# Sliding-window attention with a dense layer: 75 of TensorE's waits stand at earlier products

## The chip, the cores and the metric

The kernel runs on one core of a Trainium2 chip. The metric is the device time of one execution in microseconds (us). Three runs of the kernel before gave 438.73, 439.21 and 439.93 us; their median, 439.21 us, is the time that the change is measured against.

## The reference

Two kinds of layer alternate, each twice over the same 2048 rows of 512 numbers, all in bf16: an attention with 32 heads of 16 and a causal window of 256 rows, and a dense layer with 1792 hidden columns. Cut to what matters:

```python
scores = einsum("bhqd,bhkd->bhqk", q, k) * (Dh ** -0.5)
mask = (i - j >= 0) & (i - j < 256)
p = softmax(where(mask, scores, -1e9))
o = einsum("bhqk,bhkd->bhqd", p, v)            # then o @ wo

x = x + A(layernorm(x))       # wqkv, window attention, wo
x = x + B(layernorm(x))       # gelu(x @ w1 + b1) @ w2 + b2
x = x + A(layernorm(x))
x = x + B(layernorm(x))
```

## The kernel before, in words

The rows are cut into 16 tiles of 128, two tiles make a block, and since both pairs of layers run over all rows there are 16 blocks (`NB`) for the attention. Layers are interleaved: while the attention of one block runs, the dense layer of earlier blocks and the layernorms and projections of later ones are worked off beside it.

Four kinds of product stand on TensorE (PE):
- dense products (`pe_group`, L666): projections to Q, K and V (`xnTA`, `Wqkv_sb`), the output projection (`Wo_sb`, `OT`), and the two products of the dense layer (`W1`, `W2`, both named `W_sb` in the profile, with `xnTB` or `gT`). They use the whole array of 128x128 and stream 512 or 256 columns;
- scores (`sc`, L767): K by Q with 32 rows of the array each, four side by side;
- products with V (`pv`, L819): the masked exponentials `E` by V, 64 rows by 17 columns of the array each, 128 of them in a row (64 in the first block of a layer). V lies there twice, as `Va` and shifted by half a tile as `Vs`;
- a few transposes (L652).

ScalarE (ACT) takes the exponentials out of PSUM (L774), VectorE (DVE) and GpSimd (POOL) multiply the masks in (L795), DVE turns the products with V out of PSUM (L828), POOL helps with the layernorm (L624, L630) and the normalisation (L836). SyncE (SP) issues the DMAs: the shifted copies `Vs<-Va` (L715), the transposes of the normalised rows (`xnTA<-xn`, `xnTB<-xn`, L645) and the loads and stores.

Nothing is scheduled at run time. A plan (`_Plan`) gathers some 3,080 steps as nodes with what they read and write; the table `_ORDER` gives the order in which they are issued, `_ALT` says which run on their second engine, `_BANKS` deals out the PSUM banks. `_TURNS` is a flat list of pairs of node numbers (a, z): z gets a dependency on a, by an invented resource that a writes and z reads:

```python
for a, z in zip(_TURNS[0::2], _TURNS[1::2]):
    nodes[a]["writes"] = nodes[a]["writes"] + ["turn%d" % z]
    nodes[z]["reads"] = nodes[z]["reads"] + ["turn%d" % z]
    nodes[z]["deps"].add(a)
```

The recording layer (`_Sched.op`) then goes through the nodes in `_ORDER` and works out which semaphores each has to wait for. It remembers for every engine which counts it has already waited for (`know`), and what the engine that raised that count knew itself (`snap`), so that nothing is waited for twice:

```python
for c, v in req.items():
    if self._acquire(eng, c, v):
        waits.append((c, v))
```

Each wait is recorded ahead of the node's first instruction (`e.wait_ge(s, v)`, L127). One wait rides on that instruction itself; the others become instructions of their own on the engine's sequencer (EVENT_SEMAPHORE, up to two waits each), which stand in front of it. On PE a product is a load of weights (LDWEIGHTS, engine PEld in the profile) and the matmul behind it, and the wait rides on the load. In the rows of the program's order below, "[waits ...]" names the counters that an instruction waits for, the ones in front of it included: `cnt_act`, `cnt_dve`, `cnt_pool` for the three engines, `cnt_spdma0` to `cnt_spdma7` for DMAs.

## Time and profile before

| | |
|---|---|
| median of 3 runs | 439.21 us (438.73 to 439.93) |
| profiled execution, its own time | 440.44 us |
| span in that profile, first to last instruction | 438.9 us |
| PE busy | 412.5 us, 94% |
| ACT busy | 386.6 us, 88% |
| DVE busy | 335.6 us, 76% |
| POOL busy | 209.1 us, 48% |
| mean granted TensorE clock | 0.998 |

A matmul's busy time in the profile is modelled and runs into that of the next, so a gap in PE's stream is better read from starts than from busy times: the start of a product, plus as many steps as there are products in the row, gives the time at which the next could start. A row of the timeline merges equal instructions that follow each other; its columns are the start, the time from the first start to the last end, engine, line, operation, what is written and read, shape, and the count; in brackets, how long the engine sat idle before it and what ended that. "issue" there means that the profile shows nothing that was waited for last. PEld is the load of weights, PEldq the sequencer in front of it.

### The profile page before, as it was taken

What the parts mean: (1) busy time and instruction counts of PE and PEld (TensorE: products, weight loads), DVE (VectorE), ACT (ScalarE), POOL (GpSimd) and SP (SyncE); (2) the same over time, 40 slices, a digit from 0 to 9 for tenths busy, and PEclk for the clock granted to TensorE, in tenths of its full rate; (3) what the DMA queues carried; (4) which work ended last, traced back from release to release, by engine and by line L of the source; (5) the groups of instructions that cost most, each with busy time, mean ns of one, the idle gap of its engine ahead of it and who ended that gap; (6) DMA issues with size and microseconds to landing.
All of it is one profiled execution on the core that took longest, in us unless ns stands there. A gap on an engine that the chain in (4) does not pass through costs nothing.

```text
span 438.9 us, 16863 instructions
## 1 busy us (share of the span) xinstructions
PE 412.5 (94%) x7497; PEld 227.9 (52%) x7571; DVE 335.6 (76%) x635; ACT 386.6 (88%) x458; POOL 209.1 (48%) x233
## 2 busy tenths in 40 slices
PE   8989999998699988999999999999999999999995
PEld 4555756554444544454454455454564554444662
DVE  6999878689867788976899687878877586655841
ACT  3999988999999899999999999999889989899442
POOL 4675263372555366731566344442443645635140
PEclk9999999999999999999999999999999999999999
DMA  7782812102300303212040111201322013003030
GB/s 234 216 210 39 221 32 52 38 21 40 58 3 13 52 4 46 32 34 44 10 94 2 25 27 28 52 1 33 43 55 50 1 31 82 7 0 76 3 108 25
DMA packets 49060, 23.51 MB, mean 54 GB/s; under 512 B 34268, under 2 KB 48988, under 8 KB 48988
## 3 DMA queue, kind: packets, MB, share of 16 engines
q1 hardware_dynamic: 48988, 22.43, 23.2%
q8 instruction: 60, 0.98, 1.0%
q14 instruction: 12, 0.10, 0.1%
HBM read 8.00 MB, written 2.10 MB: 23 GB/s over the span
## 4 chain that ended last, share of the span: by engine, by line
PE 76%; ACT 10%; DVE 6%; DMA 3%; issue 3%; POOL 1%; SPq 1%; POOLq 0%; DVEq 0%
PE ps L666 59%; ACT E L774 9%; PE ps L767 9%; PE ps L819 7%; DVE OD L828 1%; DVE KT L700 1%; POOL E L795 1%; DMA xnTA<-xn 1%; DMA xnTB<-xn 1%; DVE X L911 1%; DVE stat L618 1%; SPq L645 1%; ACT Va L609 0%; DMA X<-in_A_x_dram 0%; DVE E L795 0%
## 5 line engine op out<-in xcount | busy, mean ns | idle before, releaser
L774 ACT ACTIVATE E<-ps 128x1024 bf16<-128x1024 f32 x300 | 284.0, 1038 | 21.7 <-PE ps L767 20.2
L795 POOL TENSOR_TENSOR E<-E,mask 128x512 bf16<-128x512 bf16 (+2 forms) x112 | 121.6, 1097 | 107.7 <-ACT E L774 43.8
L666 PE MATMUL ps<-W_sb,gT 128*128 128x512 bf16 x415 | 106.5, 380 | 3.2 <-issue 2.5
L666 PE MATMUL ps<-xnTB,W_sb 128*128 128x512 bf16 (+1 forms) x542 | 105.5, 335 | 3.6 <-issue 1.6
L666 PEld LDWEIGHTS ps<-xnTB,W_sb 128*128 128x128 bf16 x560 | 52.0, 98 | 43.9 <-issue 4.3
L666 PE MATMUL ps<-xnTA,Wqkv_sb 128*128 128x256 bf16 x512 | 70.6, 273 | 2.2 <-DVE OD L828 1.1
L767 PE MATMUL ps<-QT,KT 32*128 32x128 bf16 (+3 forms) x1920 | 60.6, 231 | 4.9 <-ACT E L774 2.0
L795 DVE TENSOR_TENSOR E<-E,mask 128x512 bf16<-128x512 bf16 (+2 forms) x124 | 51.2, 438 | 14.1 <-ACT E L774 6.8
L666 PEld LDWEIGHTS ps<-W_sb,gT 128*128 128x128 bf16 x448 | 39.4, 98 | 43.1 <-issue 3.4
L828 DVE STREAM_TRANSPOSE OD<-ps 128x1024 f32<-128x1024 f32 x32 | 40.0, 1249 | 23.7 <-PE ps L819 23.5
L666 PEld LDWEIGHTS ps<-xnTA,Wqkv_sb 128*128 128x128 bf16 x512 | 46.3, 98 | 22.5 <-issue 3.2
L767 PEld LDWEIGHTS ps<-QT,KT 32*128 32x128 bf16 x1920 | 28.5, 92 | 51.3 <-ACT E L774 31.0
L899 ACT ACTIVATE gT<-ps,b1T 128x512 bf16<-128x512 f32 (+1 forms) x80 | 43.7, 606 | 10.1 <-PE ps L666 10.0
L907 POOL TENSOR_TENSOR Xb<-X,b2all 128x512 f32<-128x512 bf16 x32 | 36.8, 1152 | 20.4 <-DVE X L911 11.5
L618 DVE BATCH_NORM_STATS2 stat<-X 128x6 f32<-128x512 bf16 x64 | 43.3, 684 | 2.5 <-DMA X<-in_A_x_dram 1.7
L819 PE MATMUL ps<-E,Va 64*17 64x192 bf16 (+3 forms) x1920 | 39.9, 230 | 3.0 <-ACT E L774 1.3
L700 DVE TENSOR_TENSOR KT<-ps,parmask 128x1024 bf16<-128x1024 f32 x32 | 38.6, 1211 | 5.3 <-PE ps L666 5.1
L891 DVE TENSOR_SCALAR gT<-ps,b1T 128x512 bf16<-128x512 f32 (+1 forms) x60 | 36.8, 631 | 6.3 <-PE ps L666 5.9
L836 POOL TENSOR_TENSOR Nb<-OD,Rc 128x512 bf16<-128x512 f32 x18 | 19.0, 1056 | 42.9 <-DVE Rc L832 28.6
L819 PE MATMUL ps<-E,Vs 64*17 64x128 bf16 (+3 forms) x1920 | 39.2, 230 | 0.0
L630 POOL TENSOR_TENSOR rstd<-rstd,mhalf 128x2 f32<-128x2 f32 (+1 forms) x33 | 24.3, 736 | 28.9 <-DVE rstd L624 27.2
L911 DVE TENSOR_TENSOR X<-Xb,ps 128x512 bf16<-128x512 f32 x32 | 21.6, 682 | 19.2 <-PE ps L666 19.0
(49 smaller groups left out, 362.3 us busy)
## 6 DMA issues: line engine op xcount, KB each, us to landing
Vs<-Va SPq DMA_DIRECT2D x64, 68.0 KB, 2.9
W_sb<-in_B_w_dram SPq DMA_DIRECT2D x4, 512.0 KB, 4.6
out_dram<-X SPq DMA_DIRECT2D x16, 128.0 KB, 2.0
X<-in_A_x_dram SPq DMA_DIRECT2D x3, 512.0 KB, 6.6
Wqkv_sb<-in_A_wqkv_dram SPq DMA_DIRECT2D x4, 256.0 KB, 7.3
W_sb<-in_B_w_dram SPq DMA_DIRECT2D x1, 768.0 KB
W_sb<-in_B_w_dram SPq DMA_DIRECT2D x2, 384.0 KB, 5.2
Wqkv_sb<-in_A_wqkv_dram SPq DMA_DIRECT2D x1, 512.0 KB, 6.9
```

The source lines that it names most:

```text
L618: add("dve", lambda e, B, t=t, k6=k6: e.bn_stats(stat6[:, k6, :], X[:, t, :]), reads=["X%d" % t], writes=["st%d" % k6], key="bs%d" % (k + j))
L666: r = e.matmul(ps[:, B[g][0], cols], lhsT, rhs, start=st, stop=sp)
L700: add("dve", lambda e, B, g=g, i=i: e.tensor_tensor(out=KT[:, kb, 2 * i : 2 * i + 2].rearrange("p c m a q -> p a (c m) q"), in0=ps[:, B[g] ...
L767: x = e.matmul(ps[:, bk[r], o : o + n], KT[rows, kb, c, m].rearrange("p a q -> p (a q)"), QT[rows, c, q : q + n], start=True, stop=True)
L774: add("act", lambda e, B, g_=g_, gi=gi: e.activation(E[:, 2 * gi : 2 * gi + 2, e0 : e0 + 512], ps[:, B[g_][0] : B[g_][0] + 2, :], AF.Exp, ...
L795: fn = lambda e, B: e.tensor_tensor(out=Ew, in0=Ew, in1=Mw, op=ALU.mult)
L819: x = e.matmul(ps[32 * r : 32 * r + VW, B[g][par], c % 2 * 2 * P + lo : c % 2 * 2 * P + hi], V[rows, (2 * b + m // 2) % VR, c * HC + 2 * r ...
L828: add("dve", lambda e, B: e.transpose(OD[:, s].rearrange("p a c q -> p (a c q)"), ps[:, B[g][0] : B[g][0] + 2, :]), reads=["ps:" + g], wri ...
L891: add("dve", lambda e, B, g=g, fc=fc: e.tensor_scalar(out=gT[:, fc, c0 : c0 + M], in0=ps[:, B[g][0], 0:M], scalar1=b1T[:, fc : fc + 1], sc ...
L899: add("act", lambda e, B, g=g, fc=fc: e.activation(gT[:, fc, c0 : c0 + M], ps[:, B[g][0], 0:M], AF.Gelu_apprx_tanh, bias=b1T[:, fc : fc + ...
L907: add("pool", lambda e, B, t=t, xs=xs: e.tensor_tensor(out=Xb[:, xs, :], in0=X[:, t, :], in1=b2all[:], op=ALU.add), reads=["X%d" % t, "b2a ...
L911: add("dve", lambda e, B, g=g, t=t, xs=xs: e.tensor_tensor(out=X[:, t, :], in0=Xb[:, xs, :], in1=ps[:, B[g][0], :], op=ALU.add), reads=["X ...
```

## The change

75 pairs are added to `_TURNS`. In each, the first node is one that TensorE waits for in any case at a later node, and the second is a dense product that stands ahead of that later node in `_ORDER`. The dense product now waits, and by `know` the later node no longer does. No instruction is added, left out or moved on any engine; only waits are. Of the 75, 63 are for DMAs, 7 for POOL and 5 for DVE. 54 of them stood at the first product with V of a group (19 places), 2 at scores, 19 at first products of a dense group (15 places). They now stand at 64 products of 512 columns and 11 of 256; 70 of these are not the first of their group. TensorE has 649 waits before and after. The products that carry a wait on themselves go from 436 to 511, the wait instructions that stand alone on PE at L127 from 161 to 119, 28 of the 42 in front of products with V. On SP four DMA transposes no longer wait for an earlier DMA of their own counter, because what they wait for otherwise now implies it.

```diff
@@ -358,7 +358,14 @@
     2817, 2842, 2751, 2751, 2945, 2945, 2940, 2945, 2944, 2944, 2935, 2935, 2958, 2935, 2954, 2954, 2962, 2954, 2949,
-    2995, 2889, 2995, 2906,
+    2995, 2889, 2995, 2906, 149, 233, 148, 231, 141, 168, 45, 263, 44, 246, 426, 320, 646, 537, 579, 294, 186, 293,
+    441, 301, 905, 627, 903, 625, 364, 679, 365, 678, 358, 509, 555, 742, 967, 823, 682, 862, 674, 846, 1282, 894,
...
+    2514, 2350, 2516, 2345, 2536, 2329, 2591, 2333, 2785, 2384, 2429, 2383, 2423, 2381, 2422, 2380, 2430, 2361, 2795,
+    2683, 2543, 2748, 2549, 2743, 2542, 2742, 2843, 2722, 2841, 2721, 2954, 2862, 2998, 2903,
 ]
```

The first place is PE around 186 us of the profile, ahead of a group of products with V. The diff puts seven lines into the file, so that below it L666 reads L673 in the changed kernel, L767 reads L774 and L819 reads L826. Before:

```order
L767 MATMUL ps<-QT,KT 128x256 [waits cnt_act]
L767 MATMUL ps<-QT,KT 128x256 x7
L666 MATMUL ps<-Wo_sb,OT 128x512
L666 MATMUL ps<-xnTB,W_sb 128x512 [waits cnt_dve]
L666 MATMUL ps<-xnTB,W_sb 128x512 x2
L819 MATMUL ps<-E,Va 17x64 [waits cnt_spdma7,cnt_spdma6,cnt_dve,cnt_act,cnt_spdma3,cnt_spdma0]
```

And now:

```order
L673 MATMUL ps<-Wo_sb,OT 128x512 [waits cnt_spdma0]
L673 MATMUL ps<-Wo_sb,OT 128x512 [waits cnt_dve]
L774 MATMUL ps<-QT,KT 128x256 [waits cnt_act]
L774 MATMUL ps<-QT,KT 128x256 x7
L673 MATMUL ps<-Wo_sb,OT 128x512
L673 MATMUL ps<-xnTB,W_sb 128x512 [waits cnt_dve]
L673 MATMUL ps<-xnTB,W_sb 128x512 x2
L826 MATMUL ps<-E,Va 17x64 [waits cnt_act,cnt_dve]
```

Four waits for DMAs have gone up to dense products, one to the first row shown and three to products ahead of it; at the first product with V two are left, the last of which rides on its own load, so that one separate wait remains of three.

The second place is PE around 145 us, again ahead of products with V. Before:

```order
L666 MATMUL ps<-W_sb,gT 128x512 x10
L767 MATMUL ps<-QT,KT 128x256 [waits cnt_act]
L767 MATMUL ps<-QT,KT 128x256 x7
L666 MATMUL ps<-xnTA,Wqkv_sb 128x256 x8
L819 MATMUL ps<-E,Va 17x64 [waits cnt_dve,cnt_pool,cnt_spdma0,cnt_spdma1]
```

And now:

```order
L673 MATMUL ps<-W_sb,gT 128x512 x8
L673 MATMUL ps<-W_sb,gT 128x512 [waits cnt_spdma0]
L673 MATMUL ps<-W_sb,gT 128x512 [waits cnt_spdma1]
L774 MATMUL ps<-QT,KT 128x256 [waits cnt_act]
L774 MATMUL ps<-QT,KT 128x256 x7
L673 MATMUL ps<-xnTA,Wqkv_sb 128x256 x8
L826 MATMUL ps<-E,Va 17x64 [waits cnt_pool,cnt_dve]
```

The wait for DVE stood first, in a separate instruction, with another separate one behind it; it is now the last and rides on the load.

The third place is PE around 370 us, where a wait for POOL moves. Before:

```order
L666 MATMUL ps<-W_sb,gT 128x512 x6
L767 MATMUL ps<-QT,KT 128x192 [waits cnt_act]
L767 MATMUL ps<-QT,KT 128x192 x7
L767 MATMUL ps<-QT,KT 128x128 x4
L666 MATMUL ps<-W_sb,gT 128x512 x3
L819 MATMUL ps<-E,Va 17x64 [waits cnt_spdma4,cnt_dve,cnt_spdma2,cnt_spdma7,cnt_act,cnt_spdma0,cnt_pool]
```

And now:

```order
L673 MATMUL ps<-W_sb,gT 128x512 x4
L673 MATMUL ps<-W_sb,gT 128x512 [waits cnt_spdma2]
L673 MATMUL ps<-W_sb,gT 128x512 [waits cnt_pool]
L774 MATMUL ps<-QT,KT 128x192 [waits cnt_act]
L774 MATMUL ps<-QT,KT 128x192 x7
L774 MATMUL ps<-QT,KT 128x128 x4
L673 MATMUL ps<-W_sb,gT 128x512 x3
L826 MATMUL ps<-E,Va 17x64 [waits cnt_act,cnt_dve]
```

Seven waits became two. PE asks for POOL's mask product four dense products and twelve scores earlier than it did.

## The prediction

> **What bounds the kernel now.** I read the page first, then the chain of waits, then who waited for whom on TensorE, and then PE's stream at the places that change.

> ```profile
> PE 412.5 (94%) x7497; PEld 227.9 (52%) x7571; DVE 335.6 (76%) x635; ACT 386.6 (88%) x458; POOL 209.1 (48%) x233
> PE 76%; ACT 10%; DVE 6%; DMA 3%; issue 3%; POOL 1%; SPq 1%; POOLq 0%; DVEq 0%
> PEld ps L666 <- issue: 13.0, 54, 0.8
> PEld ps L819 <- issue: 7.6, 18, 0.6
> PEld ps L767 <- issue: 7.4, 22, 0.6
> L127 PEldq EVENT_SEMAPHORE  x161: 51/51/1401, 6.1 to 420.4; - x161
> ```

> TensorE is the bound: 94% busy, 76% of the chain that ended last. So a tenth of a microsecond taken out of its stream is mostly a tenth off the end. The next rows are what could tempt one to a large forecast: the load engine idles 28 us with nothing that the profile shows to wait for, 7.6 of it in front of products with V. The last row counts the separate wait instructions on PE's sequencer, 161, mostly 51 ns each. (The third number, 1401, is one that started on its first wait and stood on its second.) But the load engine idles also because one load of weights lasts less than one product streams. What counts is whether the array itself has a hole.

> The step from one product to the next comes from rows below: four of 512 columns take 1.03 us with 0.38 for the last, so 0.216 each; eight of 256 take 1.05 with 0.27 for the last, so 0.11.

> **The change: what the moved waits cost where they stood.** First two changes from dense products to products with V, on PE: one with a single wait that rides on the load, one with seven waits, three instructions of them separate. All of these waits but those the change keeps had ended long before.

> ```profile
> 47.83 0.71 PE L666 MATMUL ps<-xnTB,W_sb 128*128 128x256 bf16 x5
> 48.47 0.24 PE L819 MATMUL ps<-E,Va 64*17 64x64 bf16 x8
> ...
> 342.65 0.81 PE L666 MATMUL ps<-W_sb,gT 128*128 128x512 bf16 x3
> 343.39 0.24 PE L819 MATMUL ps<-E,Va 64*17 64x64 bf16 x8
> ```

> Five steps of 0.11 from 47.83 end at 48.38, the product with V starts 0.09 later. Three of 0.216 from 342.65 end at 343.30; again 0.09. So 0.09 is the price of going from the whole array to the small tiles, and three separate waits add nothing to it. PE's sequencer works through them while the dense products ahead still stream. Of the 36 places that lose waits, 31 have either this gap (or none, between dense products) or a longer one caused by a wait that stays. There the change is worth 0, but for the bound on two of them below.

> The five others have more, by the same reckoning:

> ```profile
> 144.62 1.05 PE L666 MATMUL ps<-xnTA,Wqkv_sb 128*128 128x256 bf16 x8
> 145.73 0.24 PE L819 MATMUL ps<-E,Va 64*17 64x64 bf16 x8
> ...
> 185.50 0.81 PE L666 MATMUL ps<-xnTB,W_sb 128*128 128x512 bf16 x3
> 186.44 0.24 PE L819 MATMUL ps<-E,Va 64*17 64x64 bf16 x8
> ...
> 311.15 1.03 PE L666 MATMUL ps<-W_sb,gT 128*128 128x512 bf16 x4
> 312.28 0.24 PE L819 MATMUL ps<-E,Va 64*17 64x64 bf16 x8
> ...
> 404.37 0.60 PE L666 MATMUL ps<-W_sb,gT 128*128 128x512 bf16 x2
> 404.86 0.49 PE L666 MATMUL ps<-xnTB,W_sb 128*128 128x256 bf16 x3
> ...
> 406.80 0.60 PE L666 MATMUL ps<-xnTB,W_sb 128*128 128x256 bf16 x4
> 407.35 0.24 PE L819 MATMUL ps<-E,Va 64*17 64x64 bf16 x8
> ```

> Gaps 0.23, 0.29, 0.27, 0.06 and 0.11 us; less 0.09 (0 between dense products), the holes are 0.14, 0.20, 0.18, 0.06 and 0.02, together 0.60. That is all there is to win at these places.

> How much of it is the handling of waits, and how much a wait that is truly late? The rows of what was late, and of the loads that followed:

> ```profile
> 144.79 0.68 DVE L911 TENSOR_TENSOR X<-Xb,ps 128x512 bf16<-128x512 f32 x1
> L127 PEldq EVENT_SEMAPHORE  x2: 51/51/51, 145.5 to 145.6; - x2
> 145.70 0.14 PEld L819 LDWEIGHTS ps<-E,Va 64*17 64x17 bf16 x8 [0.31 <-issue]
> ...
> 185.95 0.28 DVE L795 TENSOR_TENSOR E<-E,mask 128x256 bf16<-128x256 bf16 x1
> 186.41 0.14 PEld L819 LDWEIGHTS ps<-E,Va 64*17 64x17 bf16 x8 [0.60 <-issue]
> ...
> 166.37 0.66 DVE L607 CAST QT<-ps 128x512 bf16<-128x512 f32 x1
> 167.08 0.11 PEld L666 LDWEIGHTS ps<-Wqkv_sb,xnTA 128*128 128x128 bf16 x2 [0.54 <-DVE QT L607]
> ```

> At 145 DVE ended at 145.47, then came two separate waits 0.1 apart, and the load at 145.70: 0.23 behind DVE. At 186 it is 186.23 to 186.41, 0.18. The last pair is a load whose only late wait rides on itself: 167.03 to 167.08, 0.05. So a late wait costs 0.05 on the load, and about 0.1 more for itself and for each separate wait behind it. The terms:
> - 145.7: the wait for DVE rides on the load afterwards. 0.23 less 0.05 is 0.18, the hole is 0.14: 0.14.
> - 186.4: the same, 0.18 less 0.05: 0.13 of the 0.20.
> - 312.3: a late separate wait stays, but none stands behind it: one step, some 0.08 by estimate (0.1 at most).
> - 404.9: the one separate wait goes and the late one rides on the load: 0.05.
> - 407.4: the same, but the hole is 0.02: 0.02.

> Sum 0.42 us. Bounds: at most the 0.60 of all holes, and 0.1 for two places (115.7 and 168.9) where one step may fall away behind a late exponential; at least 0, if what is late at each place comes in later by itself.

> **What they cost where they stand now.** No row shows these 75 themselves. The nearest row is the last stretch of dense products, where by the program's order 26 products wait, one of them behind a separate wait instruction:

> ```profile
> 409.47:433.80 24.33, 24.23 (x159) 1.00 0.17 49
> ```

> PE is busy for 24.23 of 24.33 us (the last columns are the clock, the DMA share and GB/s). Those 26 cost at most 0.10 in all, 0.004 each, and 75 at that rate 0.3; some of the 26 were truly late, so I take 0 for a wait that ended long before, and keep 0.3 as the bound. At each new place the thing waited for had ended 1.1 us or more before the load in the profiled execution, the least at 370.2, whose rows stand with the second rival. The cover is that lead. If it is gone, PE stands there for what is lacking, at most until where the wait stood before, and with it the scores, products with V and everything that ACT and DVE take from them.

> The four DMA transposes on SP that lose a wait lose one that had ended before what they still wait for; 0.

> The net is 0.42 off the profiled span of 438.9, with bounds of 0.7 off and 0.3 on. Does it reach the end? The pieces of the chain at the three large places are PE's own:

> ```profile
> 145.73 1.55 PE ps L819 x97
> 186.44 1.30 PE ps L819 x101
> ```

> Behind 145.7 the chain leaves PE for DVE, POOL and a DMA transpose and comes back, each released by the one before, so nothing there must swallow it. The profiled execution took 440.44 us, 1.2 more than the median of 439.21; a difference carries over, a level does not: 439.21 less 0.42 is 438.8.

> **Rivals.**

> *The separate waits cost PE their own time, hidden in places that I call normal.* 42 go. At 51 ns each that is 2.1 us: 437.1; at the 0.1 between two of them, 4.2 and 435.0. For it: 7.6 us of load idle in front of products with V, named "issue". Against it: 0.09 after three separate waits and 0.09 after none. It needs a sequencer with less lead over the array than these rows show. I take 437.1 for this rival. [...]

> *A wait that now stands too early.* Place: the dense product at 370.2, ahead of twelve scores and three more products.

> ```profile
> 368.42 0.67 POOL L795 TENSOR_TENSOR E<-E,mask 128x256 bf16<-128x256 bf16 x1 [0.53 <-DVE xn L640]
> 369.30 1.47 PE L666 MATMUL ps<-W_sb,gT 128*128 128x512 bf16 x6
> 371.79 0.25 PE L819 MATMUL ps<-E,Va 64*17 64x64 bf16 x8
> ```

> POOL's product ends at 369.09. The sixth of the six dense products will ask for it, when its weights are loaded, one step ahead of it: 4 steps after 369.30, at 370.16. The products with V asked at 371.79. If POOL ends over 1.1 us later than here, PE loses the difference, up to 1.6. From 2.7 us later on the loss is the full 1.6, less the gain of 0.4: 440.4. The last dense product ahead of 343.39 waits for POOL too, one step before the place where it did; as late there, it adds 0.2, and the rival stands at 440.6. For it: POOL is fed by DVE, and an earlier or later mask there is a matter of what DVE did first. Against it: POOL had idled 0.53 us ahead of that product, so it has no backlog, and it would have to be late in the same way in most executions.

> *The change does nothing*, because all holes are truly late work: 439.2. That is within the forecast's own range.

> **How the numbers follow.** About 0.3%, 1.3 us, is what a measurement of this kernel can tell from no change. Forecast with its neighbour of no change: 0.60, its own range 438.2 to 439.8 (the bounds and the spread of the runs before, 438.73 to 439.93). Separate waits cost: 0.27. Waits too early: 0.13. Below 437.9 counts as faster: 0.27 and some 0.03 of the forecast's case, where the gain adds up through DVE and ACT, 0.30. Above 440.5 counts as slower: most of the third case, 0.12. Between, 0.58. The range for 8 in 10 reaches down past 437.1 to 436.7, and up to 440.3.

> **What would show it.** In the profile afterwards, L127 on PE counts 119. The gaps ahead of the products with V near 145.7 and 186.4 shrink from 0.23 and 0.29 to about 0.1 and 0.16, and the one near 312 to 0.2; the one near 343 stays 0.09. Dense products that carry the new waits follow each other in steps of 0.216 and 0.11. I am wrong if products with V start less than 0.09 after dense ones, if many more than five places shrink (first rival), or if PE has new idle time at L673 put down to POOL or a DMA (second).

## The result, and the profile after

The changed kernel is slower: a median of 441.89 us (439.73 to 444.30, 9 runs) beside 439.84 (438.73 to 441.13, 9 runs) of the kernel before on the same chip, a ratio of 1.0053 with a 95% interval of 1.0027 to 1.0078. The prediction said 438.8, with a range of 436.7 to 440.3.

What it said of the waits is in the profile. Here is TensorE's stream in the changed kernel at the places of the prediction (start, time to the last end, engine, line, what is written and read, count):

```profile
145.48 1.05 PE L673 MATMUL ps<-xnTA,Wqkv_sb 128*128 128x256 bf16 x8
146.46 0.24 PE L826 MATMUL ps<-E,Va 64*17 64x64 bf16 x8
...
186.37 0.81 PE L673 MATMUL ps<-xnTB,W_sb 128*128 128x512 bf16 x3
187.17 0.24 PE L826 MATMUL ps<-E,Va 64*17 64x64 bf16 x7
...
311.55 1.25 PE L673 MATMUL ps<-W_sb,gT 128*128 128x512 bf16 x5
312.84 0.24 PE L826 MATMUL ps<-E,Va 64*17 64x64 bf16 x7
...
343.22 0.81 PE L673 MATMUL ps<-W_sb,gT 128*128 128x512 bf16 x3
343.96 0.24 PE L826 MATMUL ps<-E,Va 64*17 64x64 bf16 x8
```

By the steps of 0.11 and 0.216 the gaps are now 0.10, 0.15, 0.21 and 0.09 us; they were 0.23, 0.29, 0.27 and 0.09. And the separate wait instructions on PE:

```profile
L127 PEldq EVENT_SEMAPHORE  x119: 51/51/914, 6.1 to 406.4; - x119
```

So the mechanism is there, and yet the time went up. Who waited for whom shows where to look (what was waited for, total, times, longest):

```profile
PEld ps L673 <- issue: 11.7, 50, 0.8
PEld ps L774 <- issue: 9.4, 26, 1.3
PEld ps L826 <- issue: 7.2, 12, 2.4
```

Products with V wait for nothing that the profile names 12 times instead of 18, but the longest of these idles is 2.4 us instead of 0.6; at scores the longest is 1.3, also up from 0.6. The chain of waits shows the long one. First the kernel before, then the changed one, the same stretch:

```profile
400.91 0.15 issue
401.06 1.30 PE ps L819 x100
402.36 0.34 PE ps L767 x24
```

```profile
401.10 0.15 issue
401.25 1.26 PE ps L826 x93
402.51 2.29 issue
404.80 0.25 PE ps L826 x5
405.05 0.34 PE ps L774 x24
```

In the middle of a row of 128 products with V, at a product that has no wait at all before or after the change, PE stands for 2.29 us. The changed kernel does nothing different there. What differs is how many instructions PE has had by then. The rows of the place show that it stands between two instructions of one product: 15 loads have run, but 14 matmuls.

```profile
402.14 0.22 PEld L826 LDWEIGHTS ps<-E,Vs 64*17 64x17 bf16 x15
402.18 0.33 PE L826 MATMUL ps<-E,Vs 64*17 64x192 bf16 x14
...
404.80 0.08 PEld L826 LDWEIGHTS ps<-E,Vs 64*17 64x17 bf16 x1 [2.44 <-issue]
404.80 0.23 PE L826 MATMUL ps<-E,Vs 64*17 64x128 bf16 x2 [2.29 <-issue]
```

Section 3 of the page has the DMA queue that carries the instructions; the kernel before, then the changed one:

```profile
q8 instruction: 60, 0.98, 1.0%
```

```profile
q8 instruction: 59, 0.97, 1.0%
```

PE's program is 7571 products of two instructions (load and matmul) and 161 separate waits, some 15,300; 0.98 MB over them is 64 bytes each, and the 60 packets are of 16 KB, 256 instructions. That the changed kernel shows one packet less proves nothing: the version below with as many instructions as the kernel before shows 59 too. The numbers of the instructions say more. Counting a product as two, a separate wait as one, and from 1, the load at 404.80 (of product 7205 of 7571, counted from 0) is instruction 14,529, which is 56 times 256 and 193. The kernel before idles near 381 us at a product that has no wait of its own either:

```profile
381.49 0.82 PE L666 MATMUL ps<-xnTB,W_sb 128*128 128x512 bf16 x3 [0.19 <-issue]
```

The rivals to F: **W**, the waits cost something at the dense products where they now stand; **T**, the moved POOL waits and the four SP waits that went away shift DMAs, and the idle is a late transfer in disguise.

### The profile page after: what moved, and what is told of

It is laid out like the page before. It is cut to its first block, busy times and chain, and to the rows that moved or that the text cites. A ratio compares the mean times of both kernels' runs of the same rounds, so it can differ in the third digit from the quotient of the medians.

```text
span 440.0 us, 16817 instructions
## 1 busy us (share of the span) xinstructions
PE 412.4 (94%) x7497; PEld 228.0 (52%) x7571; DVE 335.7 (76%) x635; ACT 386.6 (88%) x458; POOL 209.4 (48%) x233
## 4 chain that ended last, share of the span: by engine, by line
PE 78%; ACT 12%; DVE 5%; issue 3%; DMA 1%; POOL 0%; SPq 0%; DVEq 0%; POOLq 0%
PE ps L673 61%; ACT E L781 11%; PE ps L774 9%; PE ps L826 8%; DVE OD L835 1%; DVE KT L707 1%; DVE X L918 1%; DVE stat L625 1%; DMA X<-in_A_x_dram 0%; DMA Vs<-Va 0%; POOL E L802 0%; ACT Va L616 0%; DVE E L802 0%; PE ps L566 0%; PE ps L659 0%
## 5 line engine op out<-in xcount | busy, mean ns | idle before, releaser
L673 PE MATMUL ps<-W_sb,gT 128*128 128x512 bf16 x415 | 106.5, 380 | 3.2 <-issue 2.5
L673 PE MATMUL ps<-xnTB,W_sb 128*128 128x512 bf16 (+1 forms) x542 | 105.3, 335 | 4.1 <-ACT E L781 2.0
L673 PEld LDWEIGHTS ps<-xnTB,W_sb 128*128 128x128 bf16 x560 | 52.1, 98 | 44.1 <-issue 3.5
L673 PE MATMUL ps<-xnTA,Wqkv_sb 128*128 128x256 bf16 x512 | 70.6, 273 | 1.8 <-DVE OD L835 1.1
L774 PE MATMUL ps<-QT,KT 32*128 32x128 bf16 (+3 forms) x1920 | 61.0, 231 | 5.6 <-ACT E L781 2.1
L673 PEld LDWEIGHTS ps<-W_sb,gT 128*128 128x128 bf16 x448 | 39.3, 98 | 43.1 <-issue 3.4
L673 PEld LDWEIGHTS ps<-xnTA,Wqkv_sb 128*128 128x128 bf16 x512 | 46.5, 98 | 21.6 <-issue 2.7
L774 PEld LDWEIGHTS ps<-QT,KT 32*128 32x128 bf16 x1920 | 28.6, 92 | 52.4 <-ACT E L781 30.1
L826 PE MATMUL ps<-E,Va 64*17 64x192 bf16 (+3 forms) x1920 | 39.7, 230 | 2.7 <-ACT E L781 1.4
L826 PE MATMUL ps<-E,Vs 64*17 64x128 bf16 (+3 forms) x1920 | 39.0, 230 | 2.3 <-issue 2.3
```

Of the source, the lines that this page charges most:

```text
L673: r = e.matmul(ps[:, B[g][0], cols], lhsT, rhs, start=st, stop=sp)
L774: x = e.matmul(ps[:, bk[r], o : o + n], KT[rows, kb, c, m].rearrange("p a q -> p (a q)"), QT[rows, c, q : q + n], start=True, stop=True)
L826: x = e.matmul(ps[32 * r : 32 * r + VW, B[g][par], c % 2 * 2 * P + lo : c % 2 * 2 * P + hi], V[rows, (2 * b + m // 2) % VR, c * HC + 2 * r ...
```

## The experiments

Inert wait instructions are used as filling: one more wait on PE for a DVE count of 1, long reached, two of them for one instruction. The edit is the same wherever they are used; only the table says how many waits stand ahead of which node (and moves the line numbers: L826 reads L837 or the like below):

```diff
         def closure(e, _fn=fn, _sems=sems, _csem=csem, _inc=inc, _pad=pad, _psem=psem):
+            for _ in range(_pad):
+                e.wait_ge(_psem, 1)
             for s, v in _sems:
                 e.wait_ge(s, v)
```

### The change, with as many instructions as before

```diff
+_PADS = {
+    227: 2, 233: 2, 246: 2, 263: 2, 319: 2, 513: 2, 514: 2, 537: 2, 662: 2, 671: 2, 877: 2, 1031: 2, 1044: 2, 1048:
...
+}
```

> The changed kernel with 42 inert wait instructions put back on PE's sequencer (a second and third wait for a DVE count of 1, satisfied since the start), each at a dense product just ahead of the place that lost one. All 75 moved waits stay where the change put them; PE's instruction number of nearly every product is again that of the kernel before (15,302 to the last product instead of 15,260). Theory F (PE's program is fetched in blocks of 256 instructions, and 42 fewer instructions shifted the block boundaries against the program): the idle of 2.5 us at 404.8 and that of 1.3 us at 54.4 are gone, the idle near 381 (0.7 us) is back, and the time is that of the kernel before less the 0.3 to 0.4 us of the wait handling: 439.5, ratio 0.999. Rival W (the waits at dense products cost PE something there) and rival T (waits for POOL and the four SP waits shift DMA traffic): the waits stand as in the changed kernel, so about 441.9, ratio 1.005.

Measured: 439.29 us (438.06 to 440.19, 12 runs) beside 439.72 of the kernel before (23 runs); ratio 0.9982, interval 0.9967 to 0.9998. The chain of waits in its profile:

```profile
399.95 1.19 PE ps L684 x5
401.13 1.24 PE ps L837 x100
402.37 0.34 PE ps L785 x24
```

The idle of 2.3 us is gone, and with all 75 moved waits in place the kernel is a little faster than before. W and T fall: they have nothing left to explain. And the idle near 381 us, which the changed kernel had lost, is back, at the same product as in the kernel before:

```profile
379.83 1.46 PE L684 MATMUL ps<-xnTB,W_sb 128*128 128x512 bf16 x6
381.49 1.04 PE L684 MATMUL ps<-xnTB,W_sb 128*128 128x512 bf16 x4 [0.20 <-issue]
```

A full step would have begun the second row at 381.13; a matmul's busy time runs into the gap, so that the idle of 0.20 that the row names is less than the 0.36 that PE loses. One thing that was not expected: scores near 53.8 us began 1.1 us behind the product ahead of them. They stand at a boundary too and have waits of their own; in the kernel before it was 0.4.

### The kernel before, moved by 64 and by 256 instructions

```diff
+_PADS = {
+    17: 16, 19: 16, 20: 16, 22: 16, 24: 16, 25: 16, 30: 16, 32: 16,
+}
```

> The kernel before, no wait moved, with 64 inert wait instructions ahead of eight of the warm-up products (2 to 4.5 us), where PE waits for the first layernorm until 5.7 us anyway. Theory F: every product's instruction number is 64 higher, the block boundaries fall 32 products earlier in the program, and with each block of 256 instructions needing about 3.5 us to be fetched some fifteen blocks that are used up faster cost time: about 19 us more by that reckoning where all of it shows, at least 8; time 448 to 459, with PE idle put down to nothing in the middle of groups of products with V or scores, the first near 39 and 52 us, others near 106, 119, 178 and 190. Rivals W and T: nothing but the instructions themselves, 64 at 51 ns under cover of 1.3 us of idle: between 0 and 2 us more, 440 to 442.

> The kernel before, no wait moved, with 256 inert wait instructions: the 64 of the second kernel and 192 more, up to three at each of 80 dense products up to 34 us. Theory F: from 34 us on all instruction numbers are exactly one block higher, so the boundaries fall on the same products as in the kernel before, and nothing changes from there on; only what the instructions cost up to 34 us shows, at most 192 times 51 ns (9.8 us) and rather 2 to 5, and from 40 us to the end the distance to the kernel before stays within 0.5 us. It should be faster than the kernel with 64 by 5 us or more. If the price is that of the instructions by number, or of any shift at all, it is slower than the kernel with 64.

Measured: with 64 instructions 472.63 us (471.06 to 473.62, 4 runs), ratio 1.074 (1.0713 to 1.0767); with 256 instructions 447.01 (446.78 to 447.31, 4 runs), ratio 1.016 (1.0136 to 1.0184). Four times the instructions cost a quarter of the time. The waits of products with V, with 64, and then with 256 (the kernel before has 7.6, 18, 0.6):

```profile
PEld ps L827 <- issue: 21.8, 25, 2.7
```

```profile
PEld ps L833 <- issue: 7.6, 18, 0.6
```

With 256 the last dense products stand 8.0 us behind those of the kernel before, and that distance is there by 58 us (7.96) and stays between 7.96 and 8.4 to the end: a shift by one whole block changes nothing behind the place where the instructions were put. With 64 the distance grows from 4.6 us at 12 us to 31.9 at 429. It grows in jumps, at products without a wait, and by 0.6 to 1.3 in each of four stretches of lower clock. Four of the thirteen jumps:

```profile
43.42 0.20 PE L827 MATMUL ps<-E,Vs 64*17 64x64 bf16 x1 [2.32 <-issue]
...
188.82 0.19 PE L827 MATMUL ps<-E,Vs 64*17 64x64 bf16 x1 [2.42 <-issue]
...
205.10 0.31 PE L775 MATMUL ps<-QT,KT 32*128 32x192 bf16 x6 [2.15 <-issue]
...
409.11 0.34 PE L827 MATMUL ps<-E,Vs 64*17 64x192 bf16 x16 [2.26 <-issue]
```

The first two places were named beforehand as near 39 and 52 us; they came at 43 and 58, behind the 4.6 of the start and, for the second, the idle at the first. Of the others named, the one near 106 did not come. My ceiling of 459 was too low by 14 us. The start is 4.6 of them. I had put the 64 waits at 51 ns each under cover; in a row of eight they cost 0.11 each (warm-up products 0.88 us apart instead of 0.43), and the first load behind them starts at 8.34 instead of 5.72, 2.6 later. The other 2.0 come by 12.1 us: up to there dense products of 256 columns still step by 0.21, and in the kernel before they step by 0.11 from the first one, at 7.30; why is not shown. The lower clock later (0.985 on average in the profile, of which more below) is some 3.5. The rest is that the idles sum to some 24 us, by the distance, instead of 19.

The one with 256 came out above the 2 to 5 us more that I thought likely for the same reasons: 4.6 of its 8.0 are there by 13 us.

This pair also measures a block. With 64 instructions there are eleven blocks that PE would have used up in 1.1 to 2.7 us (by the starts in the kernel before, its own idles taken out). Nine took 3.5 to 4.0 us, one 4.8, where the fetch began 2.0 us behind the boundary, and one no more than its 2.6, where it began 0.1 behind. Usually the packet starts 0.75 to 1.25 us behind the boundary and takes 0.9 to 1.6, and the product that waits for it starts 1.2 to 1.4 behind its end. Blocks with 3.5 us or more of work showed no idle in most cases and up to 0.5 in some.

The trace shows the size of a block, with packets of 16 KB and a remainder that returns every 256 instructions; what starts a fetch no run here shows. In this run a boundary cost nothing, or up to 0.5 us, behind blocks with 3.5 us or more of work, and 2.15 to 2.42 in the four rows above. 128 products with V, the 256 instructions of a block, start within 1.1 to 1.3 us.

### The changed kernel once more

> The changed kernel once more, beside the others on one chip. Theory F: PE again idles 1 us or more, put down to nothing, at the ninth-last but one quartet of the products with V near 404.8 us (product 7206 of 7571), and at scores near 54.4 us; time 441 to 443. If those two were an accident of one execution, they stand elsewhere or are gone, while the time is still 441 to 443.

Measured: 442.34 us (439.67 to 443.67, 12 runs), ratio 1.0059 (1.0041 to 1.0078). The idle stands at the same product, in the fastest of the twelve executions, which is the profiled one:

```profile
399.63 1.19 PE ps L826 x93
400.82 1.90 issue
402.72 0.25 PE ps L826 x5
```

The step at scores near 54 us was 0.4 here, not 1.4, so that part of the expectation failed; it varies between 0.4 and 1.1 in versions that are as fast as the kernel before, and is no part of the difference.

### Only the early pairs, only the late ones

The kernel before with the 68 pairs whose new wait stands ahead of 390 us, and with the other seven. The first, against the changed kernel:

```diff
-    2683, 2543, 2748, 2549, 2743, 2542, 2742, 2843, 2722, 2841, 2721, 2954, 2862, 2998, 2903,
+    2683,
```

> The kernel before with only the 68 pairs whose new wait stands ahead of 390 us; at the group of products with V near 404 and behind it every wait stands as before. PE has 36 instructions fewer up to there. Theory F: the boundary falls on product 7204, and PE idles there 2 us or more as in the changed kernel, though no wait near it was moved; near 381 it does not idle: 442, ratio 1.005. Rivals that look for the cause at the waits near 404: the idle is gone, 439.5, ratio 0.999.

> The kernel before with only the last 7 of the 75 pairs (new waits from 397 us on), which are all that touch the group near 404 and what follows. PE has 2 instructions fewer there. Theory F: the boundary stays at product 7186 (7185 before), no idle near 404, the one near 381 stays: 439.6, ratio 1.000. Rivals that look for the cause at the waits near 404: idle of 2 us there, 441.9, ratio 1.005.

Measured: early pairs alone 441.19 us (439.91 to 443.22, 9 runs), ratio 1.0044 (1.0023 to 1.0064); late pairs alone 438.93 (437.90 to 440.59, 12 runs), ratio 0.9992 (0.9976 to 1.0009). The kernel in which nothing is moved near 404 has the idle there, one product earlier as counted; the kernel in which only that place is changed does not have it. The chain with the early pairs alone:

```profile
399.72 1.19 PE ps L826 x92
400.91 2.32 issue
403.23 0.26 PE ps L826 x5
403.49 0.54 PE ps L774 x22
```

Its profile has something more. Busy time by stretch (us; then PE, PEld, DVE, ACT, POOL; then the granted clock, the DMA share and GB/s):

```profile
396.00:400.90 4.90, 4.90 (x151) 2.34 (x149) 1.54 (x3) 4.73 (x6) 3.69 (x5) 1.00 0.32 86
400.90:403.23 2.33, 0.01 (x2) 0.00 (x0) 0.00 (x0) 0.00 (x0) 0.89 (x1) 1.00 0.17 56
403.23:404.03 0.80, 0.80 (x36) 0.64 (x36) 0.46 (x1) 0.00 (x0) 0.00 (x0) 0.62 0.00 0
404.03:406.28 2.25, 2.25 (x8) 0.65 (x6) 2.22 (x5) 1.94 (x2) 0.00 (x0) 0.50 0.04 7
406.28:410.00 3.72, 3.72 (x39) 1.89 (x41) 2.21 (x7) 2.81 (x3) 0.00 (x0) 0.92 0.00 0
```

Behind the idle the granted clock falls to half for some 3.4 us, and dense products of 512 columns come every 0.43 us. That costs another 1.5 us: by the starts of the same products, this kernel is 1.1 behind the kernel before just after the idle, and 2.6 at the products with V that begin at 409.96 (407.35 there). It doesn't happen each time: of the 21 runs of the changed kernel 15 (4 of 9 and 11 of 12) had a mean granted clock of 0.996, as much as half the clock for some 3.5 us of 440, and 6 had 1.000; their medians are 442.8 and 441.4. The two that were profiled are among the 6, so where the lower clock lies in the 15 is taken from this profile. The 32 runs of the kernel before beside this experiment lie between 0.998 and 1.000. The lower clock followed an idle of 2.32 us in this profile and one of 1.89 in that of the last experiment (0.71 on average from 404 to 410 us), while 2.29 and 1.90 in the two profiles of the changed kernel left it at 1.000. So the length of the idle alone does not decide; what does is not shown.

### Filling at the end alone, and filling placed by block

28 instructions, one at each of 28 dense products; and 50, ten of them up to 58 us, twelve between 185 and 276, and the same 28. The expectations put the 28 between 385.9 and 392.6 or 393.7 us; in the kernel before those products stand from 387.5 to 395.3.

> The changed kernel with 28 inert wait instructions, one each at 28 dense products between 385.9 and 392.6 us (times of the kernel before); nothing else. Theory F: the block boundary that fell on product 7205, in the middle of products with V, falls 14 products earlier, and the one ahead of it in a dense stretch at about 397 us instead of at scores right ahead of the group; the idle of 2.1 to 2.5 us near 404.8 is gone, the one near 381 stays away: 442.1 less 2.3, so 439.8, ratio 1.000. Rivals W and T: the waits stand as in the changed kernel, and 28 instructions more can only cost: 442 to 444.

> The changed kernel with 50 inert wait instructions at dense products, placed so that few blocks of 256 instructions are used up in less than 4 us: 10 up to 58 us, 12 between 184 and 276, 28 between 385.9 and 393.7. Theory F: the boundaries up to 185 us lie within a product or two of those of the kernel before, the idles of 2.5 us near 404.8 and of 0.7 near 381 are both gone, and the shorter ones near 106 and 120 (0.5 and 0.3) stay: about 0.6 less than the kernel with the same count as before (439.3): 438.7, ratio 0.997. Rivals: 442 or more.

Measured: 438.96 us (437.61 to 439.97, 12 runs), ratio 0.9986 (0.9970 to 1.0002); and 438.69 (437.92 to 440.40, 12 runs), ratio 0.9990 (0.9975 to 1.0005). The kernel before had 439.41 beside them (32 runs). By the ratios, adding 28 instructions to the changed kernel makes it faster by some 3 us. In the first the row of products with V is whole again:

```profile
399.64 1.19 PE ps L683 x5
400.83 1.36 PE ps L836 x103
402.19 0.34 PE ps L784 x24
```

That the second loses neither near 381 nor near 404 is in its trace too (its largest step without a wait is 0.28 us), but it had a step of 0.96 at 54 us, at scores that stand at a boundary and have waits of their own. These versions and the one with the same count are not told apart by their intervals; only that one's lies wholly below 1.

### Why the block came so late

> The changed kernel with the three stores of finished rows that SP issues from 397.9 us on (tiles 6, 7 and 10) held back until a dense product at about 412 us; PE's instructions and their numbers are the changed kernel's. It asks why the block behind product 7205 came so late: its fetch began 2.2 and 2.8 us behind the first product of the block before it, elsewhere 0.75 to 1.25, and in that time no DMA of the stores moved either. Theory G (the fetch waited for the stores' DMAs): it begins about 1 us behind that product, and the idle near 404.8 shrinks from 2.1 to 2.5 us to about 1; with it the time to 440.5, ratio 1.002. Theory F alone, with the late fetch from another cause: the idle stays at 2.1 to 2.5 us and the time at 442, ratio 1.005. Either way the idle stays at product 7205.

```diff
-    2683, 2543, 2748, 2549, 2743, 2542, 2742, 2843, 2722, 2841, 2721, 2954, 2862, 2998, 2903,
+    2683, 2543, 2748, 2549, 2743, 2542, 2742, 2843, 2722, 2841, 2721, 2954, 2862, 2998, 2903, 2764, 2369,
```

In `_ORDER` the three stores 2369, 2386 and 2750 also move, to directly behind node 2764.

Measured: 441.00 us (439.08 to 442.68, 12 runs), ratio 1.0020 (1.0003 to 1.0036). The chain:

```profile
400.85 0.15 issue
401.00 1.26 PE ps L833 x93
402.26 1.89 issue
404.15 0.25 PE ps L833 x5
```

From 399 us to the end of the idle no packet of the data queue moved at all, and still the fetch began 2.2 us behind the first product of the block (399.58 to 401.78). Theory G falls, and it falls by the trace: the time alone would not have told, since the ratio is the 1.002 that G expected and its interval leaves out the 1.005 of the other side. 3 of the 12 runs had the lower clock, against 15 of 21, which is some 0.65 us less on average; why so few is not settled. Why the fetch is late there stays open. In four executions with this idle it began 0.8 to 1.4 us behind the group's first product with V (401.25 to 402.66, 399.63 to 400.38, 399.72 to 400.60, 401.00 to 401.78). So it may be asked for some instructions behind the boundary, after the waits at the head of the group, which stand 18 instructions behind it; that was not tried.

## Why the prediction was wrong

**What bounds the kernel.** Right: 2.3 us that PE stands at one product are 2 us at the end.

**What the waits cost where they stood.** Right, and nearly to the hundredth. By the starts of the products, the same in the changed kernel, its repetition and three kernels with filling, PE gained 0.13 us at 145.7 (predicted 0.14), 0.15 at 186.4 (0.13), 0.08 at 312.3 (0.08), 0.04 at 404.9 (0.05) and 0.02 at 407.4 (0.02): 0.42, as the sum said. With the boundaries put back, the time was 0.4 us below the kernel before by the medians, and 0.2% by the ratio.

**What they cost where they stand now.** Right: 0 for the 75. The kernel with the same count shows no loss, and the dense products follow each other in their steps.

**The rivals.** That separate waits hide a cost of 51 ns or more each in places that I called normal: wrong, the gap near 343 is 0.09 with one separate wait as with three. That a wait stands too early: not seen; no idle at L673 is put down to POOL, and PE passed the place at 370 without a gap. The chance of 0.12 for a slower kernel rested on this rival, so it did not foresee what came.

**The step that failed** is in none of these. The prediction worked out what the 42 separate waits cost as waits and, having found their cost hidden, took their removal to have no other effect. The term that was missing is that they are also 42 places in PE's instruction stream; the section on the change even says that no instruction is left out, and on PE 42 are. With its parts as the runs show them:

- the idle near 404.8 appears: 2.1 and 2.5 us in the two profiles of the changed kernel, by the distance to the kernel before ahead of it and behind it;
- the lower clock behind it: about 1.4 us in 15 of 21 runs by the medians, 1.0 on average;
- the idle near 381 shrinks: 0.4 less;
- the moved waits: 0.42 less.

That is 2.3 and 1.0 less 0.8, or some 2.5 us more, beside the measured differences of the medians of 2.05 and 2.62.

Could it have been seen beforehand? The rows were there. In the kernel before, two products without a wait began 0.7 and 0.8 us behind the one ahead, scores near 106.8 and a dense product near 381.5, and the page listed a queue named "instruction". I read the 28 us of "issue" as weight loads that take less time than a product streams (98 ns for a dense one, beside steps of 0.216 and 0.11), and did not ask at which products the long ones stand.

## What to carry to other kernels

In this kernel an edit that changed only how many instructions PE has moved everything behind it against the blocks of 256 in which they are fetched: 64 instructions more cost 33 us, 256 more, one whole block, 7 (other engines were not tried). Where short instructions stand in long rows (here 128 products with V, 256 instructions in 1.1 to 1.3 us), count instructions per stretch, and when two versions differ by idles in the middle of such a row, put the count back with inert instructions before judging the edit itself. The long idles here share three things: no wait at the product, "issue" as the cause, and one and the same remainder of the instruction's number.

## What the runs showed of the hardware that I had not expected

- Of eleven blocks of 256 instructions that PE would have used up in 1.1 to 2.7 us, ten took 3.5 us or more from one boundary to the next (nine 3.5 to 4.0, one 4.8; kernel with 64 instructions more); the four idles shown there lasted 2.15 to 2.42 us. A shift by 64 instructions cost this kernel 33 us, one by 256 cost 7, all of it by 58 us.
- Behind an idle of PE of 2.32 us the granted clock was halved for some 3.4 us (0.50 at 404 to 406 us of the kernel with the early pairs), which added 1.5 us to the 2.32; in the changed kernel's profile an idle of 2.29 us left the clock at 1.00.
- Separate waits that had long ended cost 0.11 us each where eight stand in a row (products 0.88 us apart), though the median separate wait in the kernel before is shown as 51 ns.
